# FFN backward in two passes: weight gradients from DMA-transposed gradients, then the input gradient summed in PSUM

## The chip, the cores and the metric

The kernel runs on one core of a Trainium2 chip. The metric is the device time of one execution, in microseconds. A core has five engines that run side by side: TensorE (PE, with its weight loads shown apart as PEld), VectorE (DVE), ScalarE (ACT), GpSimd (POOL) and SyncE (SP). PE multiplies out of SBUF into PSUM; ACT and DVE copy PSUM back to SBUF. DMAs are issued from the queues of SP, ACT and POOL, each in order, and are carried out by 16 shared DMA engines.

## The reference

The reference is the gradient of a block that multiplies a state-space convolution by a gated feed-forward network (FFN). Cut to the part that matters:

```python
xn = layernorm(x)                       # x: [L=2048, D=576]
gate = xn @ w1 ; up = xn @ w3           # w1, w3: [D, F=4608]
h = silu(gate) * up ; out = h @ w2      # w2: [F, D]
result = x + s(xn) * silu(out)          # s: the state-space convolution
# gradients of all parameters and of x, given grad_out [L, D]
```

With go_o the gradient at `out`, the FFN backward computes

- gh = go_o @ w2ᵀ, and from it gg = gh · up · silu'(gate) and gu = gh · silu(gate), all [L, F];
- the weight gradients hᵀ go_o (out_12, [F, D]), xnᵀ gg (out_10, [D, F]) and xnᵀ gu (out_11, [D, F]);
- the input gradient gg @ w1ᵀ + gu @ w3ᵀ, added to the convolution's input gradient and taken back through the layer norm (out_1).

All inputs and outputs are bf16; sums are f32.

## The kernel before, in words

The kernel runs in phases: layer norm, convolution, FFN forward, the backward of the convolution and of its parameters, and, from 2380 us on, the FFN backward (`phase6_ffn_bwd`, `phase6_body`) and the layer-norm backward (`phase7_ln_bwd`). Only these last two are touched. The forward has left gate and up in DRAM with F on the partitions (`G_dram`, `U_dram`, 36 F tiles of 128 x 2048), and go_o in both layouts (`GO_dram` with tokens on the partitions, `GOT_dram` with D on them). `GXN_dram` holds the convolution's input gradient.

Phase 6 walks over 12 super-blocks of three F tiles. For each F tile:

1. w2's rows are transposed by PE into `w2T` (L1178, copies at L1180), w1's and w3's columns into `w1T` and `w3T` (L1186, L1189).
2. In four pieces of 512 tokens, `ph` = w2T · go_oT (five matmuls of 512 columns, L1203), then ACT and DVE form `hT`, `guT`, `ggT` (L1206 to L1219). F is on the partitions.
3. A weight gradient is a sum over tokens, so PE needs the tokens on the partitions. For `hT`, `ggT` and `guT` in turn, PE transposes 16 blocks of 128 x 128 into PSUM (`ptr_ps`, L1232), DVE or ACT copies them to `tl` (L1235, L1237), and 32 matmuls of 288 columns sum into `pgw` (L1241), two column pieces for each token tile. The w1 and w3 gradients come out with F on the partitions and are transposed back by PE (L1254, L1257) before they are stored.

After the three F tiles of a super-block, the input gradient of all 16 token tiles is brought up to date. It lives in SBUF as f32 (`gxn`); each of the 32 pieces is multiplied by an f32 identity into `px` (L1268), six matmuls add the super-block's share (L1274), and ACT copies the sum back (L1275). When all super-blocks are done, phase 7 handles the 16 token tiles: five DVE steps over 576 columns, a load of grad_out, a store.

Engines run their instructions in program order as a scheduler laid them out from this code; buffers of a pool (`bufs`) decide how far one step may run ahead of another. DMAs by `self.dma` (L81) alternate between the queues of SP and ACT. `dpieces()` gives the two column pieces of 288; `cfg.dch` the five D chunks (four of 128 and one of 64).

Of the kernel before, what the change touches and what calls it, by code (L numbers as in the profile page):

```python
# [10 lines left out]
ACT = mybir.ActivationFunctionType  # L11
# [5 lines left out]
P = 128  # L17
# [43 lines left out]
class K:  # L61
# [1042 lines left out]
    def phase6_ffn_bwd(self):  # L1104
        nc, cfg = self.nc, self.cfg
        D, DT, L, LT, F, FT = cfg.D, cfg.DT, cfg.L, cfg.LT, cfg.F, cfg.FT
        aps = self.aps
        QW = min(512, L)
        NQ = L // QW
        SB = 3 if FT % 3 == 0 else (2 if FT % 2 == 0 else 1)  # L1110
        NSB = FT // SB
        GB = 8
        assert LT % GB == 0 or LT < GB
        GBe = min(GB, LT)
        NG = LT // GBe
        pieces = self.dpieces()
        nfull = D // P
        rem = D - nfull * P
        with self.tc.tile_pool(name="e_big", bufs=1) as big:
            gxn = self.phase6_body(big)  # L1120
            self.phase7_ln_bwd(gxn)

    def phase6_body(self, big):
# [3 lines left out]
        QW = min(512, L)  # L1127
        NQ = L // QW
        SB = 3 if FT % 3 == 0 else (2 if FT % 2 == 0 else 1)
        NSB = FT // SB  # L1130
        GB = 8
        assert LT % GB == 0 or LT < GB
        GBe = min(GB, LT)
        NG = LT // GBe
        pieces = self.dpieces()
        nfull = D // P
        rem = D - nfull * P
        with self.tc.tile_pool(name="e_wsb", bufs=2) as wsbp, \
                self.tc.tile_pool(name="e_w", bufs=2) as wp, \
                self.tc.tile_pool(name="e_gu", bufs=2) as gup, \  # L1140
                self.tc.tile_pool(name="e_q", bufs=2) as qp, \
                self.tc.tile_pool(name="e_ft", bufs=SB + 1) as ftp, \
                self.tc.tile_pool(name="e_tl", bufs=2) as tlp, \
                self.tc.tile_pool(name="e_gw", bufs=2) as gwp, \
                self.tc.tile_pool(name="e_stage", bufs=1) as stg, \
                self.tc.tile_pool(name="e_ps_h", bufs=2, space=bass.MemoryType.PSUM) as ps_h, \
                self.tc.tile_pool(name="e_ps_tr", bufs=2, space=bass.MemoryType.PSUM) as ps_tr, \
                self.tc.tile_pool(name="e_ps_gw", bufs=1, space=bass.MemoryType.PSUM) as ps_gw, \
                self.tc.tile_pool(name="e_ps_x", bufs=1, space=bass.MemoryType.PSUM) as ps_x:
            go_o = big.tile([P, LT, D], BF16, name="go_o6")  # L1150
            for i in range(LT):
                self.dma(go_o[:, i, :], self.GO_dram[:, i, :])
            go_oT = big.tile([P, DT, L], BF16, name="go_oT6")
            if rem > 0:
                nc.vector.memset(go_oT[rem:P, DT - 1, :], 0.0)
            for c, (do, dsz) in enumerate(cfg.dch):
                self.dma(go_oT[0:dsz, c, :], self.GOT_dram[0:dsz, c, :])
            gxn = big.tile([P, LT, D], FP32, name="gxn6")
            for i in range(LT):
                self.dma(gxn[:, i, :], self.GXN_dram[:, i, :])  # L1160
            for sbi in range(NSB):
                fbase = sbi * SB * P
                w1c = self.load_wcols(wsbp, aps["B_w1"], fbase, SB * P, "w1c")
                w3c = self.load_wcols(wsbp, aps["B_w3"], fbase, SB * P, "w3c")
# [3 lines left out]
                for fl in range(SB):  # L1168
# [5 lines left out]
                    if rem > 0:  # L1174
                        nc.gpsimd.memset(w2T[rem:P, DT - 1, :], 0.0)
# [219 lines left out]
```

## Time and profile before

| | us |
|---|---|
| median of 3 runs (3915.92 to 3920.1) | 3916.26 |
| profiled execution: span from first to last instruction | 3910.0 |
| PE busy | 2821.1 (72%) |
| DVE busy | 2225.3 (57%) |
| ACT busy | 1693.0 (43%) |
| POOL busy | 58.1 (1%) |
| FFN backward and layer-norm backward, 2380 to 3910 us | 1530.0 |
| of these, PE busy | 1386.2 |
| of these, ACT / DVE busy | 533.4 / 627.4 |
| one super-block (2800.82 to 2923.79) | 123.0 |

The span is the profiled execution's own time; the runs' median lies 6.3 us above it. A row of a group reads: line, engine, operation, output <- inputs, shape, count | busy time, mean ns of one | idle time of the engine ahead of them and what ended it. Matmuls overlap in the pipeline, so their mean duration is longer than the pitch at which they follow each other.

### The profile page before, as it was taken

The numbers are of one execution on the slowest core, as the hardware profiler recorded it, in microseconds if no ns is written. First come the engines' busy times: TensorE is split into PE (matmuls) and PEld (weight loads), VectorE is DVE, ScalarE is ACT, GpSimd is POOL, SyncE is SP. The second block draws the span as 40 slices with busy tenths as digits, with TensorE's granted clock in tenths as the row PEclk, the third lists the DMA queues.
The fourth block names the chain that finished last, engine by engine and source line by source line (L and its number), as shares of the span: only waits on it lengthen the run. The fifth ranks groups of instructions, "written<-read, shape, count | busy, mean of one in ns | idle before, by whom it ended". The sixth has DMA issues, their size and how long they took to land.

```text
span 3910.0 us, 57433 instructions
## 1 busy us (share of the span) xinstructions
PE 2821.1 (72%) x21730; PEld 1799.3 (46%) x21730; DVE 2225.3 (57%) x4604; ACT 1693.0 (43%) x3296; POOL 58.1 (1%) x218
## 2 busy tenths in 40 slices
PE   3999968369889766453111124999999999999997
PEld 1444425246556534342111112666666666666664
DVE  6777784823443465567999994443334433344337
ACT  2888865025445445210556551333333333333332
POOL 1000000000000000000000000000000000000000
PEclk8555558679999977776555556999999999999999
DMA  2000002065665650012333323111111111111112
GB/s 68 22 21 21 22 14 102 14 165 156 173 173 155 171 169 5 25 60 56 107 99 101 102 82 123 56 58 40 38 48 59 54 44 38 47 60 52 35 37 62
DMA packets 350327, 286.99 MB, mean 73 GB/s; under 512 B 143905, under 2 KB 330786, under 8 KB 350050
## 3 DMA queue, kind: packets, MB, share of 16 engines
q10 hardware_dynamic: 179088, 149.18, 12.7%
q1 hardware_dynamic: 170962, 134.15, 12.1%
q8 instruction: 170, 2.79, 0.3%
q14 instruction: 107, 0.88, 0.1%
HBM read 187.68 MB, written 95.52 MB: 72 GB/s over the span
## 4 chain that ended last, share of the span: by engine, by line
PE 60%; DVE 28%; DMA 5%; issue 4%; ACT 3%; ACTq 1%; SPq 0%; DVEq 0%; POOL 0%; POOLq 0%
PE pgw L1241 11%; PE px L1274 6%; PE px L1268 6%; PE o_main L714 4%; PE gu L700 4%; PE gu L697 3%; PE tau_ps L353 3%; PE e_ps L356 3%; PE dft_ps L496 3%; PE ph L1203 2%; DVE prodI L1006 2%; DVE red L1014 2%; PE gk_ps L866 2%; PE e_ps L365 2%; PE ptr_ps L1232 2%
## 5 line engine op out<-in xcount | busy, mean ns | idle before, releaser
L1241 PEld LDWEIGHTS <-tl 128*128 128x128 bf16 x3456 | 344.1, 101 | 145.6 <-DVE tl L1235 44.1
L1257 DVE COPY gw_stage<-ptr_ps 128x128 bf16<-128x128 bf16 (+1 forms) x360 | 53.3, 214 | 527.7 <-PE ptr_ps L1254 527.7
L1275 ACT COPY gxn<-px 128x288 f32<-128x288 f32 x384 | 153.5, 400 | 432.1 <-PE px L1274 401.1
L1241 PE MATMUL pgw<-xn_bf,tl 128*128 128x288 bf16 x2304 | 307.6, 286 | 6.6 <-DVE tl L1235 5.0
L1268 PE MATMUL px<-gxn,ident_f 128*128 128x288 f32 x768 | 287.4, 456 | 28.4 <-ACT gxn L1275 24.7
L1274 PE MATMUL px<-w3T,guT 128*128 128x288 bf16 x1152 | 300.6, 286 | 0.0
L1274 PE MATMUL px<-w1T,ggT 128*128 128x288 bf16 x1152 | 300.2, 286 | 0.0
L993 PE MATMUL pT<-gK,QTr 64*128 64x32 bf16 x576 | 72.6, 185 | 295.8 <-DVE QTr L979 269.5
L708 DVE TENSOR_TENSOR silu<-g_sp,sig 128x256 bf16<-128x256 bf16 x288 | 83.8, 292 | 341.8 <-ACT g_sp L705 341.3
L697 PE MATMUL gu<-xnT,w1res 128*128 128x256 bf16 x1440 | 228.7, 274 | 46.8 <-ACT u_sp L706 34.2
L704 ACT ACTIVATE sig<-gu 128x256 bf16<-128x256 f32 x288 | 110.8, 385 | 272.7 <-PE gu L700 231.2
L700 PE MATMUL gu<-xnT,w3c 128*128 128x256 bf16 x1440 | 228.5, 275 | 0.0
L993 PEld LDWEIGHTS <-QTr 64*128 64x128 bf16 x1152 | 65.0, 101 | 319.1 <-DVE QTr L979 273.7
L1241 PE MATMUL pgw<-go_o,tl 128*128 128x288 bf16 x1152 | 186.7, 317 | 25.1 <-DVE tl L1235 23.5
L1235 DVE COPY tl<-ptr_ps 128x1024 bf16<-128x1024 bf16 x108 | 73.6, 682 | 225.6 <-PE ptr_ps L1232 225.5
L1203 PE MATMUL ph<-go_oT,w2T 128*128 128x512 bf16 x720 | 183.2, 387 | 20.8 <-ACT w2T L1180 9.9
L714 PE MATMUL o_main<-w2r,hT 128*128 128x512 bf16 x576 | 185.8, 391 | 9.6 <-DVE hT L709 2.4
L1268 PEld LDWEIGHTS px<-gxn,ident_f 128*128 128x128 f32 x768 | 115.4, 188 | 129.2 <-ACT gxn L1275 124.2
L697 PEld LDWEIGHTS <-w1res 128*128 128x128 bf16 x1440 | 131.1, 98 | 71.1 <-issue 35.8
L1206 ACT ACTIVATE sig<-gate_q 128x512 bf16<-128x512 bf16 x144 | 90.8, 631 | 137.4 <-DMA gate_q<-G_dram 125.1
L700 PEld LDWEIGHTS <-w3c 128*128 128x128 bf16 x1440 | 132.7, 99 | 30.3
L1237 ACT COPY tl<-ptr_ps 128x1024 bf16<-128x1024 bf16 x108 | 109.4, 1013 | 85.3 <-PE ptr_ps L1232 62.7
(356 smaller groups left out, 6834.4 us busy)
## 6 DMA issues: line engine op xcount, KB each, us to landing
rep_t<-RT_dram SPq DMA_DIRECT2D x72, 256.0 KB, 4.0
rep_r<-RT_dram ACTq DMA_DIRECT2D x72, 256.0 KB, 3.6
gate_q<-G_dram SPq DMA_DIRECT2D x144, 128.0 KB, 2.2
up_q<-U_dram ACTq DMA_DIRECT2D x144, 128.0 KB, 2.2
w2r<-in_B_w_dram ACTq DMA_DIRECT2D x108, 144.0 KB, 2.6
w2r<-in_B_w_dram SPq DMA_DIRECT2D x72, 144.0 KB, 2.3
w3c<-in_B_w_dram SPq DMA_DIRECT2D x72, 128.0 KB, 2.5
w3c<-in_B_w_dram ACTq DMA_DIRECT2D x72, 128.0 KB, 3.3
```

Of the source, the lines that this page charges most:

```text
L353: nc.tensor.matmul(pt[:], lhsT=self.thp[rows, c, :], rhs=SELQ[rows, cols], start=True, stop=True)
L356: nc.tensor.matmul(pe[:], lhsT=self.rho[rows, c, :], rhs=SELQ[rows, cols], start=True, stop=True)
L496: nc.tensor.matmul(pt[:, 0:pw], lhsT=mat[:, tt, kc * P:(kc + 1) * P], rhs=src_fn(tt)[:, po:po + pw], start=(tt == 0), stop=(tt == KT - 1))
L697: nc.tensor.matmul(gu[:, 0, :], lhsT=w1[:, c, f0:f0 + P], rhs=xnT[:, c, tsl], start=(c == 0), stop=(c == DT - 1))
L700: nc.tensor.matmul(gu[:, 1, :], lhsT=w3c[:, c, :], rhs=xnT[:, c, tsl], start=(c == 0), stop=(c == DT - 1))
L714: nc.tensor.matmul(o_main[ts][:, 0:pw], lhsT=hT[:, ts * P:(ts + 1) * P], rhs=w2r[:, po:po + pw], start=(fi == 0), stop=(fi == FT - 1))
L993: nc.tensor.matmul(pT[:, gi, kind, :], lhsT=lhs[rows, dl, :], rhs=rhs[rows, dp, :], start=True, stop=True)
L1203: nc.tensor.matmul(ph[:], lhsT=w2T[:, c, :], rhs=go_oT[:, c, qs], start=(c == 0), stop=(c == DT - 1))
L1241: nc.tensor.matmul(pgw[pi_][:, 0:pw], lhsT=tl[:, k * P:(k + 1) * P], rhs=rhs_src[:, tt, po:po + pw], start=(tt == 0), stop=(tt == LT - 1))
L1268: nc.tensor.matmul(px[:, 0:pw], lhsT=self.ident_f[:], rhs=gxn[:, ts, po:po + pw], start=True, stop=False)
L1274: nc.tensor.matmul(px[:, 0:pw], lhsT=lw, rhs=rh, start=False, stop=(idx == len(mm) - 1))
L1275: nc.scalar.copy(out=gxn[:, ts, po:po + pw], in_=px[:, 0:pw])
```

## The change

The two phases become two passes with nothing kept in SBUF from one to the other.

*Pass 1* (`phase6_weights`) walks over 18 groups of two F tiles and works on whole rows of 2048 tokens. ACT computes silu and its derivative directly (`Silu`, `Derivative_silu`), with one copy of ph in pieces of 1024. `hT`, `guT`, `ggT` and w2's rows are no longer transposed by PE: four DMA transposes per F tile on SP's queue (`nat_transpose`) write them to SBUF with the tokens (for w2: D) on the partitions. With `gu_n` and `gg_n` of two F tiles side by side (256 columns) and xn as the stationary operand, the w1 and w3 gradients come out as [D, F] and need no transpose back; the last 64 rows of D of both share one PSUM tile, one in each half. The gradients of a group are issued after the elementwise work of the next. gg and gu also go to DRAM (`GG_dram`, `GU_dram`), by stores on ACT's queue. Loads of gate, up and w2 and the stores of weight gradients are issued by POOL.

*Pass 2* (`phase6_inputs`) has all of w1 and w3 in SBUF, transposed by 72 DMA transposes straight from DRAM, loads gg and gu in eight chunks of 256 tokens, and sums each token tile over all 36 F tiles in PSUM (`px`, 144 matmuls) before one add of the convolution's gradient. The f32 identity matmuls and the copies back are gone. The layer-norm backward of a token tile follows right behind it, with the first sum moved to ACT.

```diff
-                self.tc.tile_pool(name="e_ft", bufs=SB + 1) as ftp, \
-                self.tc.tile_pool(name="e_tl", bufs=2) as tlp, \
...
-                    for (srcT, rhs_src, kind) in ((hT, go_o, "w2"), (ggT, self.xn_bf, "w1"), (guT, self.xn_bf, "w3")):
...
-                                nc.tensor.transpose(ptt[:, k * P:(k + 1) * P], srcT[:, tt * P:(tt + 1) * P], self.ident_bf[:])
...
-                for ts in range(LT):
-                    for pi_, (po, pw) in enumerate(pieces):
-                        px = ps_x.tile([P, 512], FP32, name="px")
-                        nc.tensor.matmul(px[:, 0:pw], lhsT=self.ident_f[:], rhs=gxn[:, ts, po:po + pw], start=True, stop=False)
...
+    def nat_transpose(self, dst, src):
+        self.nc.sync.dma_start_transpose(out=dst, in_=src)
...
+                self.tc.tile_pool(name="e_in", bufs=2) as inp, \
+                self.tc.tile_pool(name="e_el", bufs=2) as elp, \
+                self.tc.tile_pool(name="e_t", bufs=2) as tp, \
+                self.tc.tile_pool(name="e_hn", bufs=3) as hnp, \
+                self.tc.tile_pool(name="e_nat", bufs=2) as natp, \
...
+            for gi in range(NGRP + 1):
+                if gi < NGRP:
+                    tiles = self.phase6_elementwise(gi, GRP, wp, inp, elp, tp, hnp, natp, ps_h, go_oT)
+                if gi > 0:
+                    self.phase6_weight_grads(gi - 1, GRP, prev, go_o, gwp, ps_w2, ps_gw)
+                prev = tiles
...
+            nc.gpsimd.dma_start(out=gate[:], in_=self.G_dram[fi])
+            nc.scalar.activation(out=silu[:], in_=gate[:], func=ACT.Silu)
...
+            self.nat_transpose(h_n[:], hT[:])
...
+            self.nat_transpose(w2T[:], w2r[:])
...
+            nc.vector.tensor_tensor(out=guT[:], in0=gh[:], in1=silus[fl][:], op=ALU.mult)
+            self.nat_transpose(gu_n[:, :, fl * P:(fl + 1) * P], guT[:])
+            nc.vector.tensor_tensor(out=ggT[:], in0=gh[:], in1=dsls[fl][:], op=ALU.mult)
+            self.nat_transpose(gg_n[:, :, fl * P:(fl + 1) * P], ggT[:])
+            nc.scalar.dma_start(out=self.GU_dram[:, :, fi, :].rearrange("c p l -> p c l"),
+                                in_=guT[:].rearrange("p (c l) -> p c l", l=self.TC6))
...
+        for (nat, oname) in ((gu_n, "out_11"), (gg_n, "out_10")):
+            for c in range(nfull):
+                pw_ = ps_gw.tile([P, 512], FP32, name="pgw13")
+                for tt in range(LT):
+                    nc.tensor.matmul(pw_[:, 0:GW], lhsT=self.xn_bf[:, tt, c * P:(c + 1) * P], rhs=nat[:, tt, :],
+                                     start=(tt == 0), stop=(tt == LT - 1))
...
+            nc.tensor.matmul(pw_[0:rem, 0:GW], lhsT=self.xn_bf[:, tt, nfull * P:D], rhs=gg_n[:, tt, :],
+                             start=(tt == 0), stop=(tt == LT - 1))
+            nc.tensor.matmul(pw_[rem:P, 0:GW], lhsT=self.xn_bf[:, tt, nfull * P:D], rhs=gu_n[:, tt, :],
+                             start=(tt == 0), stop=(tt == LT - 1))
...
+                nc.scalar.dma_start(out=ggc[:], in_=self.GG_dram[tc_])
+                nc.scalar.dma_start(out=guc[:], in_=self.GU_dram[tc_])
+                if tc_ == 0:
+                    for fi in range(FT):
+                        for (w, wT) in (("B_w1", w1T), ("B_w3", w3T)):
+                            self.nat_transpose(wT[:, fi:fi + 1, :], aps[w][:, fi * P:(fi + 1) * P])
...
+                    for fi in range(FT):
+                        for ai, (act, wT) in enumerate(((ggc, w1T), (guc, w3T))):
                             for pi_, (po, pw) in enumerate(pieces):
+                                nc.tensor.matmul(px[pi_][:, 0:pw], lhsT=act[:, fi, k * P:(k + 1) * P],
+                                                 rhs=wT[:, fi, po:po + pw], start=(fi == 0 and ai == 0),
+                                                 stop=(fi == FT - 1 and ai == 1))
...
+        nc.scalar.activation(out=t[:], in_=g, func=ACT.Copy, scale=-invD, accum_out=mg[:])
```

How the scheduler lays this out is seen at three places. On the queue of SP in the middle of the old phase 6, where it stood between other loads and stores (gate_q is a piece of the gate, gw_stage holds finished weight gradients):

```order
L81 DMA w3c<-in_B_w_dram 64x384
L81 DMA gate_q<-G_dram 128x512 x4
L81 DMA out_dram<-gw_30024 128x576
L81 DMA out_dram<-gw_stage 64x384 x2
L81 DMA gate_q<-G_dram 128x512 x4
```

and in the middle of the new pass 1:

```order
L1114 DMA_TRANSPOSE h_n<-hT_23025 128x16x128
L1114 DMA_TRANSPOSE w2T<-w2r_23414 128x5x128
L1114 DMA_TRANSPOSE gu_n<-guT 128x16x128
L1114 DMA_TRANSPOSE gg_n<-ggT 128x16x128
L1114 DMA_TRANSPOSE w2T<-w2r_23452 128x5x128
L1114 DMA_TRANSPOSE h_n<-hT_23032 128x16x128
L1114 DMA_TRANSPOSE gu_n<-guT 128x16x128
L1114 DMA_TRANSPOSE gg_n<-ggT 128x16x128
```

SP's queue now holds transposes alone in pass 1, one behind the other, with the w2T of a later group between the gu_n and gg_n of this one.

On PE in the middle of the old phase 6, a piece where the gradients of one F tile (pgw) and the update of the input gradient (px) meet:

```order
L1241 LDWEIGHTS tl
L1241 MATMUL pgw_31985<-xn_bf,tl 128x288
L1268 MATMUL px<-gxn_22547,ident_f 128x288
L1274 LDWEIGHTS ggT
L1274 MATMUL px<-w1T,ggT 128x288
L1274 LDWEIGHTS guT
L1274 MATMUL px<-w3T,guT 128x288
```

and in the new program at the turn from pass 1 to pass 2:

```order
L1246 LDWEIGHTS xn_bf
L1246 MATMUL pgw_29277<-gu_n,xn_bf 64x256
L1289 LDWEIGHTS ggc
L1289 MATMUL px_29418<-w1T,ggc 128x288
L1289 LDWEIGHTS ggc
L1289 MATMUL px_29419<-w1T,ggc 128x288
L1289 LDWEIGHTS ggc
L1289 MATMUL px_29584<-w1T,ggc 128x288
```

The px matmuls have moved from every super-block to one stretch behind all weight gradients; the first needs a loaded chunk (ggc) and a transposed weight (w1T).

On ACT at the same turn:

```order
L1229 CAST gw_29113<-pgw_29079 128x288
L1229 CAST gw_29113<-pgw_29080 128x288
L1273 DMA ggc<-GG_dram 128x9216
L1274 DMA guc<-GU_dram 128x9216
L81 DMA go_29422<-in_grad_out_dram 128x576
L1273 DMA ggc<-GG_dram 128x9216
```

The first chunk's loads stand behind ACT's last copies of pass 1; before, no such load existed, as gg and gu stayed in SBUF.

332 lines of the change are left out of this document (150 added, 182 removed).

## The prediction, made before the changed kernel was run

> **What bounds the kernel now.** I read the page's slices first, then a table by stage (the stretch from the last store of the scan's parameter gradients, 2380 us, to the end), then one steady super-block of three F tiles inside it.
>
> ```profile
> span 3910.0 us, 57433 instructions
> PE   3999968369889766453111124999999999999997
> DVE  6777784823443465567999994443334433344337
> PEclk8555558679999977776555556999999999999999
> DMA  2000002065665650012333323111111111111112
> 2380.00:3910.00 1530.00, 1386.21 (x9861) 919.20 (x9861) 627.41 (x1954) 533.37 (x1169) 15.04 (x54) 0.97 0.18 54
> 2800.82:2923.79 122.97, 114.35 (x827) 76.28 (x825) 47.41 (x154) 44.65 (x98) 1.42 (x5) 0.99 0.16 48
> ```
>
> The last two rows give, after the length of the stretch, the busy time of PE, PEld, DVE, ACT and POOL, the granted clock, the DMA share and GB/s. From slice 25 on PE is busy nine tenths or more, at a clock of 0.97 to 0.99; DVE, ACT and DMA are far below. So the 1530 us that the diff rewrites are bound by PE, and only 123.0 - 114.4 = 8.6 us in 123.0 (7%) of a super-block are gaps. A change pays here by taking instructions off PE, as long as nothing else becomes slower than what is left.
>
> ```profile
> L1241 PE MATMUL pgw<-xn_bf,tl 128*128 128x288 bf16 x2304 | 307.6, 286 | 6.6 <-DVE tl L1235 5.0
> L1241 PE MATMUL pgw<-go_o,tl 128*128 128x288 bf16 x1152 | 186.7, 317 | 25.1 <-DVE tl L1235 23.5
> L1274 PE MATMUL px<-w3T,guT 128*128 128x288 bf16 x1152 | 300.6, 286 | 0.0
> L1268 PE MATMUL px<-gxn,ident_f 128*128 128x288 f32 x768 | 287.4, 456 | 28.4 <-ACT gxn L1275 24.7
> L1203 PE MATMUL ph<-go_oT,w2T 128*128 128x512 bf16 x720 | 183.2, 387 | 20.8 <-ACT w2T L1180 9.9
> 2380.00:3910.00 1530.00, 230.00 (x2613) 172.00 (x818) 142.47 (x283) 0.97 0.18 54
> ```
>
> The means (286 ns) overlap in the pipeline, so I price matmuls by the pitch at which one run starts after another. The sixth row is the same stretch for the tile ptr_ps alone (PE, DVE, ACT): 230 us of PE transposes and 314 us of their copies out of PSUM.
>
> **The change, part by part.** Pitches come from the timeline of PE:
>
> ```profile
> 2808.60 3.84 PE L1203 MATMUL ph<-go_oT,w2T 128*128 128x512 bf16 x17
> 2812.28 0.61 PE L1232 MATMUL ptr_ps<-ident_bf,hT 128*128 128x128 bf16 x8
> 2848.84 4.09 PE L1241 MATMUL pgw<-go_o,tl 128*128 128x288 bf16 x32
> 2852.77 1.06 PE L1232 MATMUL ptr_ps<-ident_bf,ggT 128*128 128x128 bf16 x16
> 2867.35 0.75 PE L1268 MATMUL px<-gxn,ident_f 128*128 128x288 f32 x2
> 2867.94 0.29 PE L1274 MATMUL px<-w1T,ggT 128*128 128x288 bf16 x1
> 1004.07 0.71 PE L697 MATMUL gu<-xnT,w1res 128*128 128x256 bf16 x5
> 1004.61 0.71 PE L700 MATMUL gu<-xnT,w3c 128*128 128x256 bf16 x5
> ```
>
> 512 columns: 3.68/17 = 0.216 us. 288: 3.93/32 = 0.123. 256: 0.54/5 = 0.108. The f32 add of gxn: 0.59 per pair, 384 of them, 227 us.
>
> *Removed from PE:* those 227 us and the 230 us of transposes. *Kept:* ph, 720 x 0.216 = 156 us; gw2, 1152 x 0.123 = 141; px, 2304 x 0.123 = 283. *Changed:* the w1/w3 gradients now have 18 groups x 128 matmuls of 256 columns, 2304 x 0.108 = 249 us, and 576 with 64 output rows, 62 us at the full pitch and 31 if the two halves run side by side; I take 62, since no row shows two halves at once. Pass 1 is then 156 + 141 + 249 + 62 = 608 us of PE, 16.9 per F tile, or 18.1 with today's 7% of gaps; pass 2 is 16 token tiles of 144 x 0.123 = 17.7 us.
>
> *What must keep up with 18.1 us per F tile.* ACT and DVE, from these rows:
>
> ```profile
> L1206 ACT ACTIVATE sig<-gate_q 128x512 bf16<-128x512 bf16 x144 | 90.8, 631 | 137.4 <-DMA gate_q<-G_dram 125.1
> L1237 ACT COPY tl<-ptr_ps 128x1024 bf16<-128x1024 bf16 x108 | 109.4, 1013 | 85.3 <-PE ptr_ps L1232 62.7
> L277 ACT ACT_TABLE_LOAD x37 | 47.5, 1283 | 0.7
> L1275 ACT COPY gxn<-px 128x288 f32<-128x288 f32 x384 | 153.5, 400 | 432.1 <-PE px L1274 401.1
> L1211 DVE TENSOR_TENSOR hT<-silu,up_q 128x512 bf16<-128x512 bf16 x134 | 56.2, 420 | 3.0 <-DMA up_q<-U_dram 1.7
> gate_q<-G_dram SPq DMA_DIRECT2D x144, 128.0 KB, 2.2
> ```
>
> ACT gets two activations of 2048 elements (1013 + 2 x 382 = 1.78 us each), two copies of ph (1.01 each), two of gw2 (0.40, as L1275's) and one table load: 7.7 us. DVE gets four products of 2048 (at most 4 x 0.42 = 1.7 each) and 4.5 copies: some 9 us. Both are hidden behind PE; without that cover they would be 280 and 320 us. The stores of guT and ggT now wait on ACT's queue for DVE's products, 3.4 us, with the copies of the next ph behind them; ph has two PSUM buffers, and PE has 4.3 us of ph plus the gradients of the group before to go on with, so I cost it at nothing, and at 3.4 x 36 = 122 us if PE ran dry. On SP the same products hold up gu_n and gg_n, and behind them w2T, which ph needs; a group of lead covers it. POOL issues nine DMAs per F tile, which no row shows; from nothing up to the 2.2 us in which today's 128 KB loads land, that is 0 to 20 us, and I take 9 (hidden).
>
> *The DMA transposes* are the unknown: per F tile three of 512 KB and one of 160 KB, all on SP's queue, plus 72 of 144 KB ahead of pass 2. The trace has none. Prices per packet come from two stretches:
>
> ```profile
> DMA packets 2346, 5.69 MB, mean 335 GB/s; under 512 B 268, under 2 KB 396, under 8 KB 2345
> q1 hardware_dynamic: 1204, 2.92, 52.5%
> q10 hardware_dynamic: 1141, 2.75, 49.3%
> DMA packets 56448, 32.72 MB, mean 164 GB/s; under 512 B 33173, under 2 KB 56424, under 8 KB 56424
> q1 hardware_dynamic: 27504, 15.77, 29.8%
> q10 hardware_dynamic: 28920, 16.66, 29.6%
> ```
>
> The first (2388 to 2405 us, loads of gxn) has 16 engines x 17 us / 2346 = 116 ns per packet of 2.4 KB. The second (900 to 1100 us) has 0.594 x 16 x 200 / 56448 = 33.7 ns per packet of 580 bytes. A line through both is 7.8 ns + 0.0446 ns per byte: 19 ns for 256 bytes, 31 for 512, 190 for 4 KB. With T the time of one 512 KB transpose on the 16 engines, a low bound is T = 2048 packets of 256 bytes x 19.2 / 16 = 2.5 us; a high one, if a transpose is written in 32-byte pieces (a guess), is 16384 x 9.2 / 16 = 9.4 us. Two-byte pieces (262144 x 7.8 / 16) would make it 128 us; I give that almost no weight. The other DMA per F tile costs two loads of 512 KB (1.52 each), two stores in 512-byte runs (1.96 each), weights and outputs 2.1: 9.1 us. DMA total per F tile is 9.1 + 3.31 T: 17.4 us at T = 2.5, 40 at 9.4. So even the cheapest transpose leaves DMA about level with PE, where it now has a share of 0.18. I take T near the low end (about 3), because the bytes read are as many as in those 256-byte loads: 19 us per F tile, 684 us.
>
> The Trainium skill (DMA: Bandwidth & Descriptors, Latency and other measured facts) gives 261 GB/s for a DMA transpose; by it T is an estimated 2.0 us, PE sets the pace at 18.1, and the span is about 3398. No run here shows it yet.
>
> *Ends.* Two rows of the chain of waits (first and last) and one of the timeline:
>
> ```profile
> 2365.49 14.38 DMA out_dram<-gl_bf
> 2394.13 1.88 PE L1203 MATMUL ph<-go_oT,w2T 128*128 128x512 bf16 x4 [6.43 <-DMA go_oT<-GOT_dram]
> 3906.49 0.82 DVE o L1308
> ```
>
> the first row is what the queue of SP waits for ahead of the new phase; the first ph stays near 2390. Then 12 us to fill the first group. Between the passes the first chunk (2 x 2.36 MB at 335 GB/s, 14 us) is loaded after the last stores of pass 1 (3 us): 17 us with PE empty. The 72 weight transposes (576 source rows each, so 0.28 T: 61 us, with the second chunk's 14 beside them, 75) pace the first token tile; the second is partly hidden (17 left), then 14 x 17.7 = 248. Today's layer-norm pass at the end moves under px; what is left is one tile's chain, two copies' worth of adds (0.8), four DVE steps of at most 0.82 and the 3.5 us from the third row to the span's end: 8.
>
> Sum: 2390 + 12 + 684 + 17 + 75 + 17 + 248 + 8 = 3451 us of span; with T left open it is 3034 + 139 T (119 T in pass 1, 20 T in the weight transposes). The runs' median, 3916.3, lies 6 us over the profiled span of 3910.0, so the time is 3457; I say **3460 us**.
>
> **Rivals.**
> *DMA paces pass 1.* At T = 4.8, between the bounds, an F tile takes 25 us, and 3034 + 139 x 4.8 = 3701 us of span, 3707 as a time. For it: level already at the low bound. Against: DMA reached 335 GB/s above.
> *The transposes cost more than PE gains (slower).* 3034 + 139 T passes 3910 at T = 6.3 us, so from there on the change loses; at 9.4 us it gives 4341, or 4347 as a time. For it: by the line a 32-byte piece still costs 9.2 ns, half of a 256-byte packet, and DMA has no reserve. Against: the same bytes as packets of 256 cost a quarter.
> The Trainium skill (VectorE: DVE Perf Modes, The three transpose paths) gives 1309 ns for one 128x128 DMA transpose and 390 ns on PE. Here PE did 16 in 0.89 us (2852.77 to the next run), 56 ns each, so the skill's numbers are not rates here on PE; but 16 blocks one after another would be an estimated 21 us for T, over 5900 us in all.
> *POOL paces pass 1* by nine issues at 2.2 us: 19.8 us per F tile, 713 us, 3486. *PE alone*, with T under 2.7: 36 x 18.1 = 652, and 3414 at T = 2.5.
> *The change doesn't move the time*: it needs T within 0.06 us of 6.3.
>
> **How the numbers follow.** PE and DMA level, T up to 3.6, PE alone and POOL's case included: 0.58, from 3340 to 3540. DMA-paced, T from 3.6 to 6.3: 0.26, up to 3908. Slower: 0.14. No change: 0.02, where 0.2% (8 us) is what a measurement of this kernel can tell. Faster is 0.58 + 0.26 = 0.84. The low end, 3340, is PE alone without gaps and with the halves side by side (3414 - 44 - 31); the high end, 3830 (T = 5.7), leaves out the slower case and the top of the DMA-paced one, together with the rest under the low end about 0.2.
>
> **What would show it.** Right: no ptr_ps, weight-gradient matmuls at a pitch of 0.108, a DMA share of 0.8 to 1 in pass 1, an F-tile period near 19 us, from the last of pass 1 to the end near 365 us. DMA-paced: PE with gaps ended by DMA gu_n, gg_n or w2T. Wrong altogether: SP's 512 KB transposes over 6.3 us apart, or ACT idle behind its own stores of guT and ggT while ph waits for its copies.

## The result, and the profile after

The changed kernel takes 3572.99 us (median of 4 runs, 3569.79 to 3577.02) beside 3916.09 us for the kernel before (3915.72 to 3920.1): a ratio of 0.9123, with a 95% interval from 0.911 to 0.9136. That is 343 us less, where the prediction's 3460 us would have been 456 less. Its profiled execution has a span of 3567.9 us, 117 us over the forecast sum of 3451:

| part | forecast, us | profiled, us | difference |
|---|---|---|---|
| up to the first ph | 2390 | 2402.9 | +13 |
| pass 1, with its fill (12 + 684) | 696 | 794.2 | +98 |
| from the end of pass 1 to the end | 365 | 370.8 | +6 |

The first rows of the page of the changed kernel (span, then 40 slices):

```profile
span 3567.9 us, 49552 instructions
PE   2999994846887978455431111117777877773999
DMA  2000000207566565201133333239998889967442
```

PE, which stood at nine tenths or more from the 26th slice to the last but one in the kernel before, now stands at 7 to 8 tenths in pass 1 (from slice 28), and at 9 only in the last three; the DMA row has gone from 1 to 8 or 9 in most slices of the pass. The table by stage of the changed kernel, for pass 1, for the rest, and for one steady group of two F tiles (length; busy time of PE, PEld, DVE, ACT, POOL; clock, DMA share, GB/s):

```profile
2402.90:3197.10 794.20, 629.53 (x4752) 456.60 (x4752) 230.57 (x303) 267.27 (x247) 175.34 (x350) 0.89 0.91 200
3197.10:3567.90 370.80, 289.92 (x2309) 227.54 (x2304) 62.79 (x129) 12.42 (x32) 1.08 (x2) 0.89 0.46 153
2833.50:2877.80 44.30, 35.52 (x267) 25.62 (x266) 12.99 (x17) 15.36 (x14) 9.99 (x20) 0.88 0.89 199
```

A group takes 44.3 us, 22.1 per F tile, against 19 forecast. PE is idle for 8.8 us of it. The DMA share of 0.91 looks like the forecast's picture, an engine near its limit; the experiments show that it is not the limit. PE's timeline of that group says where PE stands still:

```profile
2833.45 8.81 PE L1196 MATMUL ph<-go_oT,w2T 128*128 128x512 bf16 x40
2842.10 4.08 PE L1225 MATMUL pgw<-go_o,h_n 128*128 128x288 bf16 x32
2846.02 5.08 PE L1237 MATMUL pgw<-gu_n,xn_bf 128*128 128x256 bf16 x45
2850.93 4.08 PE L1225 MATMUL pgw<-go_o,h_n 128*128 128x288 bf16 x32
2854.85 2.24 PE L1237 MATMUL pgw<-gu_n,xn_bf 128*128 128x256 bf16 x19
2865.75 10.15 PE L1237 MATMUL pgw<-gg_n,xn_bf 128*128 128x256 bf16 x64 [8.66 <-DVE gw L1240]
2875.83 0.30 PE L1244 MATMUL pgw<-gg_n,xn_bf 128*64 128x256 bf16 x1
2875.83 0.30 PE L1246 MATMUL pgw<-gu_n,xn_bf 128*64 128x256 bf16 x1
2875.96 0.27 PE L1244 MATMUL pgw<-gg_n,xn_bf 128*64 128x256 bf16 x1
```

One gap per group, before the second half of the w1/w3 gradients, and DVE's copy of a finished gradient (gw, L1240) ends it. On the queues of SP, POOL and DVE, in the same stretch (one fence for each engine; where an engine waited, the time and what ended the wait stand in brackets):

```profile
2840.28 4.22 SPq L1114 DMA_TRANSPOSE gu_n<-guT  x1
2844.59 7.96 SPq L1114 DMA_TRANSPOSE gg_n<-ggT  x1
2852.73 1.98 SPq L1114 DMA_TRANSPOSE w2T<-w2r  x1
2854.80 3.10 SPq L1114 DMA_TRANSPOSE gu_n<-guT  x1
2857.99 3.43 SPq L1114 DMA_TRANSPOSE h_n<-hT  x1
```

```profile
2857.60 0.15 POOL L1187 MEMSET w2r<- 128x64 bf16 x1 [15.78 <-DMA w2T<-w2r]
...
2858.64 1.08 POOL L1241 DMA_DIRECT2D out_dram<-gw  x2
```

```profile
2864.14 1.23 DVE L1178 TENSOR_TENSOR hT<-silu,up 128x2048 bf16<-128x2048 bf16 x1 [14.00 <-DMA h_n<-hT]
2865.28 0.42 DVE L1240 CAST gw<-pgw 128x256 bf16<-128x256 f32 x1
...
2873.51 0.42 DVE L1240 CAST gw<-pgw 128x256 bf16<-128x256 f32 x1 [3.73 <-DMA out_dram<-gw]
```

SP issues its transposes one by one, and in these rows each issue holds its queue for 2 to 8 us. Behind this group's gu_n and gg_n stand the second w2T and the h_n. For the first waits POOL's memset of a w2r buffer, with the stores of gradients behind it; for the other waits DVE's next hT (two buffers), with the copies of gradients behind it; and for those copies waits PE, with the next group's ph behind. That ph makes the next gu_n: the loop is closed, from 2833.45 to 2877.70. The waits of the whole of pass 1 in the changed kernel (total us, times, longest):

```profile
POOL w2r L1187 <- DMA w2T<-w2r: 342.5, 34, 19.5
DVE hT L1178 <- DMA h_n<-hT: 192.3, 14, 15.6
PE pgw L1237 <- DVE gw L1240: 137.2, 25, 10.3
DVE gw L1240 <- DMA out_dram<-gw: 122.3, 58, 15.6
```

The DMA view of pass 1 in the changed kernel (queue: packets, MB, share of the 16 engines):

```profile
q1 hardware_dynamic: 254140, 63.83, 49.1%
q10 hardware_dynamic: 74880, 37.75, 18.4%
```

q1 is the queue with the transposes: 63.83 MB in 254140 packets, 251 bytes each, and 0.491 x 16 x 794.2 / 254140 = 24.6 ns per packet. So a DMA transpose moves packets of some 256 bytes, as the low bound had it, and a 512 KB transpose costs T = 2048 x 24.6 / 16 = 3.1 us of the engines, where "about 3" was taken. The Trainium skill (DMA: Bandwidth & Descriptors, Latency and other measured facts) gives 261 GB/s for a DMA transpose with a non-contiguous middle dimension, an estimated 2.0 us; here it is 512 KB in 3.1 us, 167 GB/s, and the trace does not agree. q10 holds the 512-byte stores of guT and ggT: 0.184 x 16 x 794.2 / 74880 = 31.2 ns each, for 31 forecast.

At the turn, PE's timeline and then the chain of waits of the changed kernel:

```profile
3238.30 1.12 PE L1289 MATMUL px<-w1T,ggc 128*128 128x288 bf16 x4 [40.98 <-DMA ggc<-GG_dram]
3258.77 0.66 PE L1289 MATMUL px<-w3T,guc 128*128 128x288 bf16 x2 [19.35 <-DMA guc<-GU_dram]
```

```profile
2382.20 17.74 DMA w2r<-in_B_w_dram
...
3273.02 1.27 SPq L1114
...
3287.10 7.15 DMA w3T<-in_B_w_dram
3294.29 266.46 PE px L1289 x2159
```

(The first row of the chain is the load ahead of the first ph.) PE is empty for 60 us where 17 were forecast, but the end is set by the last w3T, which lands at 3294.3; 15 of the 16 token tiles are still to do by then (2159 matmuls, 266 us).

### The profile page after: what moved, and what is told of

It is laid out like the page before. It is cut to its first block, busy times and chain, and to the rows that moved or that the text cites. A ratio compares the mean times of both kernels' runs of the same rounds, so it can differ in the third digit from the quotient of the medians.

```text
span 3567.9 us, 49552 instructions
## 1 busy us (share of the span) xinstructions
PE 2351.2 (66%) x18910; PEld 1562.0 (44%) x18910; DVE 1893.9 (53%) x3074; ACT 1444.8 (40%) x2403; POOL 221.3 (6%) x518
## 4 chain that ended last, share of the span: by engine, by line
PE 50%; DVE 26%; DMA 8%; issue 6%; SPq 5%; ACT 2%; POOL 1%; ACTq 1%; DVEq 0%; POOLq 0%
PE px L1289 7%; SPq L1114 5%; PE o_main L714 4%; PE ph L1196 4%; PE gu L700 4%; PE gu L697 4%; PE tau_ps L353 4%; PE pgw L1237 4%; PE e_ps L356 3%; PE dft_ps L496 3%; DVE prodI L1006 2%; PE gk_ps L866 2%; DVE red L1014 2%; DMA out_dram<-gw 2%; PE e_ps L365 2%
## 5 line engine op out<-in xcount | busy, mean ns | idle before, releaser
L1237 PEld LDWEIGHTS <-xn_bf 128*128 128x128 bf16 x2304 | 241.4, 105 | 192.7 <-issue 148.7
L1289 PE MATMUL px<-w1T,ggc 128*128 128x288 bf16 x1152 | 238.3, 289 | 48.6 <-DMA ggc<-GG_dram 41.0
L708 DVE TENSOR_TENSOR silu<-g_sp,sig 128x256 bf16<-128x256 bf16 x288 | 83.8, 292 | 341.5 <-ACT g_sp L705 341.0
L1289 PE MATMUL px<-w3T,guc 128*128 128x288 bf16 x1152 | 238.2, 289 | 25.3 <-DMA guc<-GU_dram 19.4
L1237 PE MATMUL pgw<-gg_n,xn_bf 128*128 128x256 bf16 x1152 | 161.6, 310 | 136.7 <-DVE gw L1240 136.5
L1199 ACT CAST gh<-ph 128x1024 bf16<-128x1024 f32 x72 | 71.1, 1013 | 441.5 <-PE ph L1196 378.9
L1178 DVE TENSOR_TENSOR hT<-silu,up 128x2048 bf16<-128x2048 bf16 x36 | 44.1, 1224 | 236.8 <-DMA h_n<-hT 192.3
L1240 DVE CAST gw<-pgw 128x256 bf16<-128x256 f32 x144 | 60.6, 422 | 192.9 <-DMA out_dram<-gw 122.3
L1289 PEld LDWEIGHTS <-ggc 128*128 128x128 bf16 x1152 | 113.8, 99 | 79.4 <-issue 49.6
L1225 PE MATMUL pgw<-go_o,h_n 128*128 128x288 bf16 x1152 | 147.4, 286 | 0.0
L353 PE MATMUL tau_ps<-SELQ,thp 64*128 64x512 f32 x144 | 143.2, 1096 | 0.3 <-ACT WiT L242 0.3
```

What stands on the lines that cost most here:

```text
L353: nc.tensor.matmul(pt[:], lhsT=self.thp[rows, c, :], rhs=SELQ[rows, cols], start=True, stop=True)
L1225: nc.tensor.matmul(pgw[pi_][:, 0:pw], lhsT=h_ns[fl][:, tt, :], rhs=go_o[:, tt, po:po + pw], start=(tt == 0), stop=(tt == LT - 1))
L1237: nc.tensor.matmul(pw_[:, 0:GW], lhsT=self.xn_bf[:, tt, c * P:(c + 1) * P], rhs=nat[:, tt, :], start=(tt == 0), stop=(tt == LT - 1))
L1289: nc.tensor.matmul(px[pi_][:, 0:pw], lhsT=act[:, fi, k * P:(k + 1) * P], rhs=wT[:, fi, po:po + pw], start=(fi == 0 and ai == 0), stop=(fi ...
```

## The experiments

All ratios are to the kernel before, timed on the same chip; the changed kernel stands at 0.9123. Its pass 1, unchanged, took 794 to 805 us in four profiled kernels, so differences of 10 us in pass 1 are not read. Pass 1 below is the time from the first ph to the last gradient matmul. It and the rest come from the one profiled execution of each kernel, the ratio from the median of four. For the three queue edits the profiled execution was the fastest of four that lie 31 us apart (3483.34 to 3514.26), so its pass 1 of 697 us flatters it.

| kernel | median, us | ratio (95%) | pass 1, us | rest, us |
|---|---|---|---|---|
| changed | 3572.99 | 0.9123 (0.911 to 0.9136) | 794 | 371 |
| three queue edits | 3494.51 | 0.8946 (0.8917 to 0.8974) | 697 | 374 |
| no h_n transposes | 3529.85 | 0.9015 (0.9002 to 0.9028) | 740 | 379 |
| no gate and up loads | 3558.78 | 0.9091 (0.9078 to 0.9105) | 786 | 370 |
| four tiles at the turn | 3596.26 | 0.9192 (0.9179 to 0.9206) | 797 | 390 |
| hT buffers alone | 3624.95 | 0.924 (0.9199 to 0.928) | 846 | 373 |
| chunk loads on POOL | 3589.14 | 0.9153 (0.9138 to 0.9169) | 799 | 376 |
| four tiles, loads on POOL | 3554.69 | 0.9066 (0.9049 to 0.9083) | 805 | 341 |
| queue edits and turn | 3478.11 | 0.8871 (0.8849 to 0.8893) | 724 | 342 |
| gradient buffers alone | 3564.51 | 0.9105 (0.9092 to 0.9118) | 777 | 379 |
| no memset alone | 3582.41 | 0.9146 (0.9133 to 0.9159) | 791 | 374 |
| all, h on PE | 3410.12 | 0.8713 (0.87 to 0.8725) | 659 | 340 |
| all, h on PE, stores on POOL | 3470.49 | 0.8862 (0.8845 to 0.8879) | 710 | 338 |

**What sets the pace of pass 1: the DMA engines or the queues?** Theory D says the DMA engines, 0.9 busy; theory Q says the loop of queues described above.

First, DMA work taken away from a queue that is not SP's: gate and up are loaded once, and every F tile works on that pair. This kernel leaves out the other loads and so does not compute the block's gradients.

```diff
-            gate = inp.tile([P, L], BF16, name="gate6")
-            nc.gpsimd.dma_start(out=gate[:], in_=self.G_dram[fi])
+            if gi == 0 and fl == 0:
+                self.gate_0 = inp.tile([P, L], BF16, name="gate6")
+                nc.gpsimd.dma_start(out=self.gate_0[:], in_=self.G_dram[fi])
+            gate = self.gate_0
```

(and the same for up)

> gate and up are loaded once, and every F tile works on the same pair (all results of the pass are then wrong): two 512 KB loads per F tile less, 256 packets x 190 ns / 16 = 3.0 us of the DMA engines, taken from POOL's queue. SP's series of transposes and the buffers of hT and the gradients stay. Theory D: 36 x 3.0 = 108 us less, near 3465 us, as where the h_n transposes are left out. Theory Q: SP's series and the waits behind it stay, 3540 to 3575 us.

Its pass 1 in the table by stage:

```profile
2404.80:3190.90 786.10, 628.25 (x4752) 457.22 (x4752) 231.31 (x303) 268.07 (x248) 138.20 (x281) 0.89 0.79 157
```

The DMA share falls from 0.91 to 0.79 and the rate from 200 to 157 GB/s, and the pass is as long as before within what differs from run to run (786 against 794 to 805 us). Theory D falls: the DMA engines do not set the pace.

Second, nearly the same DMA work taken from SP's queue. This kernel leaves out the transposes of h after the first group, and so does not compute out_12:

```diff
-            h_n = hnp.tile([P, LT, P], BF16, name="h_n")
-            self.nat_transpose(h_n[:], hT[:])
+            if gi == 0:
+                h_n = hnp.tile([P, LT, P], BF16, name="h_n")
+                self.nat_transpose(h_n[:], hT[:])
+                self.h_0 = h_n
+            h_n = self.h_0
```

> The h_n transposes are left out after the first group (out_12 is then wrong): one 512 KB transpose per F tile less, on SP's queue and on the DMA engines (2048 packets x 24.7 ns / 16 = 3.2 us), PE's work unchanged. Theory D: the F-tile period falls from 22.1 to about 19, 36 x 3.2 = 114 us less, near 3460 us. Theory Q: a quarter of SP's serial issue goes, and hT waits for no transpose, so the period falls too, to PE's 18.1 us: about 3430 us. Alone it only prices one transpose; against the next kernel, which takes nearly the same DMA time from another queue, it tells the theories apart.

Pass 1 is 54 us shorter, 1.5 us per F tile: more than the same bytes gave on POOL's queue, but half or less of what either theory had put. What was left there was the other wait: over 500 us in the middle of pass 1 the gradient copies waited 173.0 us for their own stores, where in the changed kernel it had been 69.5.

Third, the waits taken away: more buffers for the gradients and for hT, and no memset on POOL.

```diff
+                self.tc.tile_pool(name="e_ht", bufs=4) as self.htp, \
+                self.tc.tile_pool(name="e_gw13", bufs=8) as gwp13, \
...
+            self.w2rs = [big.tile([P, DT * P], BF16, name=f"w2r6_{j}") for j in range(4)]
+            for w2r in self.w2rs:
+                nc.vector.memset(w2r[:, D:DT * P], 0.0)
...
-            hT = elp.tile([P, L], BF16, name="hT6")
+            hT = self.htp.tile([P, L], BF16, name="hT6")
...
-            w2r = wp.tile([P, DT * P], BF16, name="w2r6")
-            nc.gpsimd.memset(w2r[:, D:DT * P], 0.0)
+            w2r = self.w2rs[fi % 4]
...
-                gw = gwp.tile([P, GW], BF16, name="gw13")
+                gw = gwp13.tile([P, GW], BF16, name="gw13")
```

> Three queue waits of pass 1 are taken away together: eight buffers for the stored w1/w3 gradients (2 before), four for hT (2 before), and four w2r buffers zeroed once ahead of the pass, so that no memset on POOL waits for a w2T transpose. The bytes and packets of the DMAs stay as they are. Theory Q (the period of 44.2 us per group is a loop of queues: PE waits for the gradient copies on DVE, which stand behind hT, which waits for the h_n transposes on SP, and POOL's stores stand behind the memset): the gaps of 8 to 9 us per group close until the DMA's own 20.1 us per F tile or PE's 18 are reached, so 36 x 2.1 = 75 to 36 x 4 = 144 us less: 3430 to 3500 us. Theory D (the DMA engines, 0.9 busy, set the pace, and the buffers only hand their lateness on): within 20 us of the changed kernel, 3555 to 3575 us.

Pass 1 in the table by stage, then PE's two largest waits after the start and DVE's for its stores, with these three edits:

```profile
2411.10:3107.80 696.70, 616.39 (x4752) 448.66 (x4752) 234.09 (x303) 266.50 (x247) 168.51 (x314) 0.94 1.12 227
```

```profile
PE pgw L1229 <- ACT gw L1233: 55.0, 12, 11.2
PE pgw L1241 <- DVE gw L1244: 7.1, 4, 2.5
DVE gw L1244 <- DMA out_dram<-gw: 1.3, 1, 1.3
```

The bytes are the same, and the pass is 97 us shorter, at 227 GB/s; the medians lie 78 us apart. PE's wait for DVE's gw is down from 137.2 us to 7.1, DVE's wait for its stores from 122.3 to 1.3. This is theory Q's outcome, at its upper end. The DMA share is 1.12: the packets of several queues overlap in the records, so a share near 1 was never a full engine here. And the 20.1 us of DMA per F tile that the expectation took as a floor is none: the pass ran at 19.4. What PE waits for now is ACT: its copy of the w2 gradient stands behind stores of guT on ACT's queue.

**Which of the three waits?** Each was then taken away alone.

> Only hT gets four buffers (2 before); the gradients' two buffers and the w2r memset on POOL stay. The three waits of theory Q were taken away together before, for 78 us. If DVE's hT, waiting 14 to 16 us per group for an h_n transpose with the gradient copies behind it, is the wait that PE feels, most of it comes from here: 60 to 78 us less than the changed kernel, 3495 to 3515 us. If POOL's memset and the gradients' buffers each carry a share, a third to a half: 3535 to 3550 us.

> Only the stored w1/w3 gradients get eight buffers (2 before); hT keeps two and the w2r memset stays on POOL. With hT's buffers alone the pass became 52 us longer: DVE's gradient copies then waited 216 us (of 500) for their own stores, which stand on POOL behind the memset that waits for w2T. If that chain (SP's w2T, POOL's memset, the stores, two buffers, DVE's copy, PE) is the loop that sets the period, cutting it at the buffers gives most of what the three edits gave together: pass 1 near 710 to 740 us, 3490 to 3525 us in all. If DVE's hT, which waits 14 us per group for h_n with the copies behind it, is a loop of its own as long as the other, cutting one leaves the period: 3555 to 3580 us.

> Only the memset goes: four w2r buffers, zeroed once ahead of the pass; the gradients and hT keep two buffers. POOL still waits for w2T before it loads a w2r again, but two F tiles later. If the memset's wait was the head of the loop, the stores come out in time and the pass is as with more gradient buffers: 3490 to 3525 us. If POOL waits as long for the load as it did for the memset (10 us per F tile where all three edits are in), little changes: 3550 to 3580 us.

The edits are the three parts of the diff above. None alone gives a gain beyond the intervals, and the hT buffers alone make the pass 52 us longer. (With the gradients' buffers alone pass 1 is 17 us shorter in the profiled execution, and the median 8 us.) The waits of pass 1 show why; for hT's buffers alone, then the gradients' alone, then no memset:

```profile
POOL w2r L1188 <- DMA w2T<-w2r: 358.6, 34, 19.4
DVE gw L1241 <- DMA out_dram<-gw: 342.5, 64, 17.6
PE pgw L1238 <- DVE gw L1241: 162.6, 33, 7.7
```

```profile
DVE hT L1179 <- DMA h_n<-hT: 204.8, 15, 14.5
PE pgw L1238 <- DVE gw L1241: 125.1, 15, 9.1
```

```profile
POOL w2r L1190 <- DMA w2T<-w2r: 330.9, 32, 20.6
DVE hT L1181 <- DMA h_n<-hT: 185.6, 14, 14.4
PE pgw L1239 <- DVE gw L1242: 129.7, 25, 9.0
```

With hT free, the gradient copies wait for their stores for 342.5 us in place of 122.3. With the gradients free, the same copies still stand behind DVE's hT, which waits 204.8 us. Both waits end at the same instruction, DVE's gw, and both begin at the same place, SP's series of gu_n and gg_n; removing one leaves the other. That is the second case expected for the gradients' buffers (a loop of its own as long as the other), and its range holds. The time without the memset lies 2 us above the second case expected for it, and the hT buffers missed both of theirs. Taking the memset away changes nothing, because the load of w2r, which stands behind it, then waits for a w2T transpose just as long (330.9 us). With all three edits POOL's load still waits 349.5 us. So it is likely that the two buffer sizes worked together and the third edit gave little; that pair without the third was not run, and this is not shown. Of the 52 us that hT's buffers alone lose, the traces account for most: PE waits for DVE's gw 33 times and 162.6 us in place of 25 times and 137.2, in the steady groups twice, some 6 and some 5 us, where the changed kernel has one gap of some 8, and it is busy for 653 us in place of 630, at a lower clock (0.87 for 0.89). Why the stores then land so late is not settled.

**The turn.** Four token tiles at once when pass 2 begins (st holds tile k of chunk j, for the first two chunks):

```diff
+                    for fi in range(FT):
+                        for ai, wT in enumerate((w1T, w3T)):
+                            for si, (j, k) in enumerate(st):
+                                for pi_, (po, pw) in enumerate(pieces):
+                                    nc.tensor.matmul(pxs[si][pi_][:, 0:pw], lhsT=ch[j][ai][:, fi, k * P:(k + 1) * P],
+                                                     rhs=wT[:, fi, po:po + pw], start=(fi == 0 and ai == 0),
+                                                     stop=(fi == FT - 1 and ai == 1))
```

> Pass 2 begins with four token tiles at once (two chunks, eight PSUM banks), so that PE has four tiles' work for each transposed weight slab while SP issues the 72 weight transposes; pass 1 is unchanged. In the changed kernel PE is empty for 61 us and then works one token tile in the time of the transposes, with 15 tiles (266 us) left after the last. If the transposes (1.26 to 1.31 us each on SP, 72 x 1.3 = 94 us) set that stretch whatever PE does, 12 tiles are left after the last w3T, 3 x 17.7 = 53 us less: 3520 us. If the two extra loads of a chunk (4.7 MB) come late beside the transposes, the first tiles are not done by the last w3T, and half of that or less is gained: 3545 to 3570 us.

Neither: 19 us more behind pass 1. The first px starts 41 us after the end of pass 1, as in the changed kernel; the loads of the two chunks were issued on ACT at 3235, 3257, 3280 and 3292 us, so the second chunk's tiles came last. Next, the first two chunks' loads on POOL's queue, alone and with the four tiles:

```diff
-                nc.scalar.dma_start(out=ggc[:], in_=self.GG_dram[tc_])
+                eng = nc.gpsimd if tc_ < 2 else nc.scalar
+                eng.dma_start(out=ggc[:], in_=self.GG_dram[tc_])
```

> Pass 1 unchanged; the loads of the first two chunks go from ACT's queue to POOL's. Theory C: on ACT the first load is issued only at 3229 us and the second at 3250, though the last store of pass 1 is out at 3202, because a load there waits for landings of weight transposes that have nothing to do with it (SP and ACT share the counters of their DMAs); POOL's DMAs have counters of their own. Then the first px starts near 3215 instead of 3238, two token tiles are done by the last w3T instead of one, and one tile of 17.7 us is saved: about 3555 us. Theory S: SP's issue of the transposes alone sets that stretch (one token tile is ready when the last w3T lands, whenever it started), no change within 8 us: 3565 to 3580 us.

> Four token tiles at once at the start of pass 2, which alone cost 23 us, now with both chunks' loads on POOL's queue. Theory C: the four loads are out by 3205 and landed by about 3245, so that PE works the four tiles (71 us) beside the transposes, and 12 tiles are left at about 3300; less the 13 us in which PE waits for the third chunk, whose buffers come free only then: 3300 + 13 + 12 x 17.7 + 8 = 3533, so 3530 to 3545 us. Theory S': the four tiles cannot keep up with anything but the transposes, and the loss of 23 us stays: near 3595 us.

The chains of waits of these two kernels, loads alone first:

```profile
3309.66 2.83 DMA w3T<-in_B_w_dram
3312.53 267.15 PE px L1290 x2159
```

```profile
3313.81 4.95 PE px L1303 x39
3321.21 12.15 DMA guc<-GU_dram
3333.40 214.11 PE px L1303 x1723
```

On POOL the loads are out 6 us after the end of pass 1, and PE starts 15 us after it in place of 41. Alone that gains nothing: the same 2159 matmuls are left when the last w3T lands. That is theory S: SP's issue of the transposes sets the stretch (1.27 us in the row of the turn above, 72 of them, 105 us from first to last in the changed kernel) and one tile is done by its end. (The time, 3589 us, lies 9 us above that theory's range; pass 1 had ended 14 us later than in the changed kernel.) With four tiles at once the earlier start counts: 1723 matmuls, 12 tiles, are left, and the rest of the kernel is 341 us instead of 371. A 12 us wait for the third chunk, whose buffers come free only with the block, is in that. This is theory C's mechanism; the time, 3555 us, lies 10 us above its range, as pass 1 ended only at 3213.7 us.

Why ACT issued the first load only 32 us after the pass can be read from the semaphores in the changed kernel's trace (a semaphore is a counter that a DMA raises when it has landed, and for which a queue can wait). It is as the expectation had it: the DMAs of SP and ACT raise the same eight semaphores, those of POOL eight others. ACT's first load uses semaphore 102; a w3T transpose on 102 landed at 3228.31 us, and the load went out at 3228.86. The second uses 101; a w3T transpose on 101 landed at 3250.27, and the load went out at 3250.30.

**Together, and the h transposes back on PE.** The queue edits and the turn, with the second chunk's tiles 12 F tiles behind the first's:

```diff
-                    for fi in range(FT):
+                    LAG = 12 if bi == 0 else 0
+                    for fo in range(FT + LAG):
                         for ai, wT in enumerate((w1T, w3T)):
                             for si, (j, k) in enumerate(st):
+                                fi = fo - LAG * j
+                                if not 0 <= fi < FT:
+                                    continue
```

> All together: the three queue waits of pass 1 taken away (alone 78 us less), four token tiles at once at the turn with the loads of both chunks on POOL, and the second chunk's tiles 12 F tiles behind the first's, so that the third chunk can load meanwhile. If the two parts add up, 3495 - 50 = 3445 us, 3430 to 3460. If the gain of the turn was only the idle DMA engines of the changed kernel's slow end of pass 1, it shrinks: 3460 to 3495 us.

The time lies in the second range, but not for its reason: the turn keeps its gain in full (342 us), and it is pass 1 that has 724 us where the same three edits had 697 before. The code of the two passes is the same. In the longer one PE waits 68.8 us for ACT's copies and 19.5 for DVE's, 26 us more than the 55.0 and 7.1 above; why these copies come later stays open. The spread of 31 us between executions of the earlier kernel is as large as the difference.

Then h by PE again, as in the kernel before, with ph in pieces of 512 to free two PSUM banks:

```diff
-            self.nat_transpose(h_n[:], hT[:])
+            for hh in range(LT // 8):
+                ptr = self.ps_tr.tile([P, 8 * P], BF16, name="ptr")
+                for j in range(8):
+                    tt = hh * 8 + j
+                    nc.tensor.transpose(ptr[:, j * P:(j + 1) * P], hT[:, tt * P:(tt + 1) * P], self.ident_bf[:])
+                nc.vector.tensor_copy(out=h_n[:, hh * 8:(hh + 1) * 8, :].rearrange("p a b -> p (a b)"), in_=ptr[:])
```

> All edits for pass 1 and the turn, and the h transposes back on PE (16 of 128 x 128 per F tile, 0.9 us of PE; two copies of 1024 columns on DVE, 0.68 us each; ph in pieces of 512 to free two banks): a quarter of SP's series and 3.2 us of DMA per F tile go. Pass 1 with all three queue edits is 697 to 723 us, 38.7 us per group with the DMA queues' share at 1.15. If what is left there is the DMA engines or SP's series, pass 1 falls to PE's time, 36 x (16.0 + 0.9) = 608 us plus 5% of gaps, 640 us: 2408 + 640 + 342 = 3390, 3375 to 3420 us. If it is ACT's gradient copies, behind stores of guT that wait to be issued (4.5 us of PE per group), no more than a few us go: 3440 to 3480 us.

Its pass 1 by stage, and two rows of PE's timeline there:

```profile
2408.70:3067.40 658.70, 624.85 (x5328) 471.37 (x5328) 274.55 (x375) 323.18 (x353) 168.93 (x314) 0.98 0.96 212
```

```profile
2717.35 7.15 PE L1247 MATMUL pgw<-gg_n,xn_bf 128*128 128x256 bf16 x64
2726.30 1.07 PE L1190 MATMUL ptr<-ident_bf,hT 128*128 128x128 bf16 x16
```

3410.12 us, a ratio of 0.8713: 4.5% under the changed kernel and within the first range expected. PE is busy for 95% of the pass, at a clock of 0.98, though it does 576 transposes more; the pass is bound by PE, at 18.3 us per F tile. SP has a quarter fewer transposes. This version beats both kernels.

Last, the stores of guT and ggT issued by POOL:

```diff
-            nc.scalar.dma_start(out=self.GU_dram[:, :, fi, :].rearrange("c p l -> p c l"),
+            nc.gpsimd.dma_start(out=self.GU_dram[:, :, fi, :].rearrange("c p l -> p c l"),
                                 in_=guT[:].rearrange("p (c l) -> p c l", l=self.TC6))
```

> The kernel with h on PE, and the stores of guT and ggT issued by POOL in place of ACT, so that ACT's copies stand behind no DMA. If ACT's queue was what is left in pass 1, its 4.5 us per group go (18 x 4.5 = 80 us at most) against the kernel with h on PE alone: 3365 to 3410 us. If not, POOL's longer queue costs as much as it saves: within 15 us of that kernel.

60 us slower than the kernel with h on PE, worse than either case expected: ACT's queue was no longer a bound there (with h on PE alone, PE has no wait for ACT's gradient copies). POOL's GU_dram stores now waited 83.8 us for guT, with loads and gradient stores behind them. Of the 51 us by which pass 1 grew, 32 are PE's wait for DVE's copies of h (51.1 us in place of 18.9) and 19 a longer busy time (643.7 for 624.9, at a clock of 0.96 for 0.98). How the longer queue of POOL delays the copies of h was not settled.

## Why the prediction was right, and where not

The forecast was the likeliest case in kind and sign, the time between 3340 and 3830, and its distance of 113 us has one main source.

- **First ph at 2390: +13.** The rule that SP's store ahead of it decides was right, but behind that store w2r's 144 KB took 17.7 us to land beside the pass's other first loads, and only then could w2T be transposed.
- **"19 us per F tile", the DMA's time: near as a sum, wrong as the pace.** T was 3.1 for "about 3", and a 512-byte packet 31.2 ns for 31; the packets of an F tile took 20.1 us in all (0.91 of 22.1). But the period was 22.1 us, and taking 3.0 us of DMA off each F tile left it there. The rival "DMA paces pass 1" with T = 4.8 gave 3707; its mechanism did not occur either, and PE's gaps were ended by DVE's gw (137.2 us), not by DMA gu_n (6.1). The share of 0.8 to 1 that I named as a sign was there, and was no proof: shares of 0.79, 0.91 and 1.12 stood beside periods of 21.8, 22.1 and 19.4 us.
- **The step that failed: "a group of lead covers it".** The prediction named the queue: products hold up gu_n and gg_n on SP, and behind them w2T; it priced that at nothing. It did not ask who waits behind the waiters: POOL's stores behind a memset, DVE's gradient copies behind hT. That term measures 97 us in the profiled executions (pass 1 of 794 against 697 us with the three edits) and 78 us between the medians. The prediction also priced SP's transposes by the DMA engines' time alone, though each holds SP's queue for 1.2 to 8 us while others are in flight, 26.6 us per group (the sum over its eight).
- **ACT's stores "at nothing", 122 us if PE ran dry:** hidden in the changed kernel, 55 us of PE's waiting once the other waits were gone.
- **POOL's nine issues:** 9 us per F tile were taken, at 1.0 each. An issue took 0.54 us (the rows of POOL above show 1.08 for two). That rival fell by its price, yet POOL's order, not its speed, was part of the loop.
- **PE's terms:** ph, 288 and 256 columns at the forecast pitches. The halves do run side by side (rows at 2875.83: a pair starts together and the next pair 0.13 us later), 31 us in place of 62. PE was nevertheless busy for 630 us, not 577 (156 + 141 + 249 + 31); the last section accounts for 35 of these 53 us.
- **After pass 1, 365 us: 371.** Right in sum, with errors that cancelled. PE was empty for 60 us, not 17, since the chunk loads came late, and the 72 transposes took 105 us by SP's issue, not 61 by the engines; but they began 15 us before pass 1 ended, and the first tile was done in their time.
- **The slower rival** (T over 6.3) fell with the packet size: 251 bytes, not 32.
- **A reading:** PE's row of the kernel before stands at 4 in slice 25 and at 9 only from the 26th to the 39th. Nothing rests on the slice.

## What to carry to other kernels

A queue in which waiting instructions stand in line is a resource like an engine: for each one that may wait, list what stands behind it and follow that to the bound engine, and price the line before pricing the transfers. Two waits that end at the same instruction may have to be removed together; each alone can show nothing, or a loss. And a DMA share near 1 says that transfers are under way, not that they set the pace: take some bytes off a queue that nobody waits for, and see whether the time moves.

## What the runs showed of the hardware

A gap on PE costs more than its length. In the changed kernel's table by stage, the granted clock in the gap of the group above and right after it:

```profile
2857.50:2865.00 7.50, 0.00 (x0) 0.00 (x0) 0.86 (x1) 0.00 (x0) 2.30 (x5) 0.74 1.03 227
2866.00:2870.00 4.00, 4.00 (x21) 2.74 (x20) 2.72 (x4) 0.00 (x0) 2.66 (x5) 0.50 1.03 196
```

After 8.66 us of idling PE works at half clock (0.50) for at least 4 us; 64 matmuls of 256 columns took 10.15 us there and 7.15 in the kernel with h on PE, where no gap precedes them. The Trainium skill (TensorE: Matmul & The Clock Gate, Part 1: The HAM clock gate) says that the array's clock falls to half after an idle window of some 3.4 us; this trace agrees. This group is a bad one: after the other gaps of 8 us and more, 64 matmuls in one run took 8.5 to 9.8 us. Over the whole pass the same 4032 gradient matmuls kept PE busy for 470.4 us in the changed kernel and 435.0 in the kernel with h on PE. By this estimate the slow clock cost some 35 us there, of the 53 by which PE's 630 us exceed the 577 forecast; the other 18 stay open.

The issue of one DMA transpose holds SP's queue: 1.26 us for 144 KB from DRAM with little else under way, 1.8 to 8.5 us for 512 KB beside other traffic, while an ordinary load of 288 KB (gx, in pass 2) took 0.32 us of it. I had priced the queue at nothing.
